# Rows of the dense part transposed by TensorE instead of VectorE, and the first block's rows kept on chip

## The chip, the core and the metric

The kernel runs on one core of one Trainium2 chip, as one launch. The metric is the device time of that launch in microseconds (us), as the median of several runs. A core has five engines that run side by side and wait for one another through semaphores: TensorE (PE in the profile; its weight loads are listed apart as PEld), VectorE (DVE), ScalarE (ACT), GpSimd (POOL) and SyncE (SP), which here only issues DMAs. PE writes to PSUM, which has eight banks of 128 x 512 floats. SBUF holds the tiles, and HBM holds the inputs, the output and the scratch tensors.

## What is computed

Two layers with the same weights, one after the other. Each is attention with 32 heads of 20 columns, then an MLP with squared ReLU. Both have a layer norm in front and a residual add behind. x is 2048 x 640 in float32, the MLP's inner width is 1536.

```python
x = x + A(layernorm(x), wqkv, wo)          # attention, 32 heads, output projection wo
x = x + B(layernorm(x), w1, b1, w2, b2)    # relu(x @ w1 + b1)**2 @ w2 + b2
x = x + A(layernorm(x), wqkv, wo)
x = x + B(layernorm(x), w1, b1, w2, b2)
```

## The kernel before

Products that need precision are made from three matmuls: each operand is split into a high part, rounded to the type that PE reads, and a low part that holds the rest. High times high, high times low and low times high are summed in PSUM. So most operands are tiles of shape [128, 2, 512]: plane 0 high, plane 1 low. `split_to` (L265) makes the two planes from a source, the high one by a cast on ACT (L267), the low one by a subtraction on DVE (L268). `THREE` (L307) names the three pairs, `chain` (L317) issues one sum of such matmuls on PE (L320).

The rows are handled in four blocks of 512 (`NQB`), each block as four tiles of 128 rows. A layer (`layer`, L1117) has these stages.

1. `qkv` (L702) and `attention` (L886): projections, scores, softmax and weighted values. Attention's own rows are normalised and transposed by `front` (L393): one PE transpose for each 128 x 128 square (L408), four of them into one PSUM bank, then a split out of PSUM. The dense part below does it in another way.
2. Output projection, `add_heads` (L1029), once for each block. For each of the four row tiles and each half of the 640 columns there is one chain of 15 matmuls into a bank, then DVE adds the bank to the residual row tile (L1044). When both halves are done, the row tile is stored to the scratch tensor `x_mid` (an issue on SP). The residual rows of the next block are loaded one block ahead (L1034).
3. MLP, `mlp` (L1069), once for each block, in two halves (`fh`) of six inner tiles. In each half: six chains of 15 matmuls from the transposed rows xnT and `w_1`; for each a ReLU on ACT (L1084), a square on DVE (L1085) and a split into h; then eight chains of 18 matmuls from h and `w_2`, each added on DVE to a row tile of the residual (L1104). That residual is loaded again from `x_mid` during the first half, and GpSimd adds `b2` to it (L1091).

Between stages 2 and 3 the rows of `x_mid` must be normalised and transposed, since the first matmuls of the MLP need them with the 640 columns on the partitions. `turned_rows` (L1048) is a generator that does this in 13 steps: load four row tiles from `x_mid`; statistics of each (`stats`, L250: L255 and L256 on DVE, L258 and L259 on GpSimd); then for each tile the normalisation (L263) and the transposition by `turned` (L284), in two steps. `turned` has 16 DVE instructions for each row tile, each of which turns five 32 x 32 squares (L292), into an SBUF tile y. `parts` (L299) splits y into xnT: for each of the five column groups a cast on ACT (L304) and a subtraction, on GpSimd or DVE in turn (L305).

The order on each engine is the order in which the program issues. `side` (L1128) takes the next step of a list and issues it; it is called after every chain of `add_heads` (8 times for a block), after every inner tile and after every chain of the second product in `mlp` (28 times for a block). So a list of steps, with `None` for an empty place, sets which work stands between which chains. Before the change, block 0's 13 steps stand in the third and fourth block of `add_heads`, and split as they go. For the other blocks the steps stand in the first half of the MLP block before, and their splits all at one place in its second half, behind the first chain of the second product (L1109).

All loads go through SP's one queue, in order (the `dma` helper, L76). The weights `w_1` (15 tiles) come in fours after each block of the projection, and its last three with `w_2` (16 tiles, L1148) after the last block; in the queue the loads of the MLP's rows stand behind them. SBUF tiles come from two rings: `arena` with 42 slots (weights, xnT, h) and `xp` with 11 row tiles (`NX`, L36), which holds x, y and r. A tile is reused when its last reader is done. PSUM banks are taken in turn (`ps_all`, L110).

Of the kernel before, what the change touches and what calls it, by code (L numbers as in the profile page):

```python
# [8 lines left out]
F32 = mybir.dt.float32  # L9
# [7 lines left out]
P = 128  # L17
# [5 lines left out]
KD = D // P  # L23
NF = F // P
QB = 512
NQB = S // QB
# [13 lines left out]
def tile_layers(  # L40
# [11 lines left out]
    nc = tc.nc  # L52
# [10 lines left out]
    def name(p):  # L63
        n_alloc[0] += 1
        return f"{p}{n_alloc[0]}"

    def slot(shape, dtype, label):
        return arena.tile(shape, dtype, tag="slot", name=name(label))

    def dma(eng, dst, src):  # L70

        if dst.dtype == F32R:
            dst = dst.bitcast(F32)
        if src.dtype == F32R:
            src = src.bitcast(F32)
        eng.dma_start(dst, src)  # L76

    def xtile(label):
        return xpool.tile([P, D], F32, tag="x", name=name(label))
# [30 lines left out]
    ps_all = Ring(0, 1, 2, 3, 4, 5, 6, 7)  # L110

    ident = cpool.tile([P, P], F32, name="ident")
# [149 lines left out]
    def normalise(eng, x, mv):  # L262
        eng.tensor_scalar(x, x, mv[:, 0:1], mv[:, 1:2], op0=ALU.subtract, op1=ALU.mult)  # L263

    def split_to(dst_hi, dst_lo, src):  # L265

        nc.scalar.copy(dst_hi, src)  # L267
        nc.vector.tensor_sub(dst_lo, src, dst_hi.bitcast(F32))  # L268
# [11 lines left out]

    def pool_lo(dst, a, b):
        nc.gpsimd.tensor_sub(dst, a, b)  # L282

    def turned(x):  # L284


        y = xtile("y")
        view = y.rearrange("p (k t) -> p k t", k=KD)
        src = x.rearrange("p (k c i) -> p c k i", k=KD, i=32)
        for a in range(4):  # L290
            for c in range(4):
                nc.vector.transpose(  # L292
                    view[32 * c : 32 * c + 32, :, 32 * a : 32 * a + 32],
                    src[32 * a : 32 * a + 32, c],
                )
            if a % 2:
                yield y

    def parts(res, i, y):  # L299

        for k, t in enumerate(res):
            cols = slice(i * P, (i + 1) * P)
            hi, lo, src = t[:, 0, cols], t[:, 1, cols], y[:, k * P : (k + 1) * P]
            nc.scalar.copy(hi, src)  # L304
            (nc.vector if k % 2 else nc.gpsimd).tensor_sub(lo, src, hi.bitcast(F32))  # L305

    THREE = ((0, 0), (0, 1), (1, 0))  # L307

    def row_tile(src, r):
        t = xtile("x")  # L310
        dma(nc.sync, t, src[r * P : (r + 1) * P, :])
        return t
# [4 lines left out]
    def chain(dst, pairs):  # L317
        last = len(pairs) - 1
        for n, (a, b) in enumerate(pairs):
            nc.tensor.matmul(dst, a, b, start=(n == 0), stop=(n == last))  # L320
# [108 lines left out]
    k_t, q_t, v_t, mx_t, kept = {}, {}, {}, {}, {}  # L429
# [596 lines left out]
        dma(q, ot.rearrange("p l t -> p (l t)"), d_o[k * P : (k + 1) * P, qb])  # L1026
        ready.setdefault(qb, {})[k] = ot

    def add_heads(qb, x_src, x_mid, xs, side):  # L1029

        ot = ready.pop(qb)
        for i in range(4):
            if qb + 1 < NQB:
                xs.append(row_tile(x_src, qb * 4 + 4 + i))  # L1034
            x = xs.pop(0)
            for hf in range(2):
                dst = ps_all("po")
                chain(dst[:, :HALF], [
                    (ot[k][:, hx, i * P : (i + 1) * P], w_o.piece(k * 4 + hw * 2 + hf))
                    for k in range(KD)  # L1040
                    for hx, hw in THREE
                ])
                c = slice(hf * HALF, (hf + 1) * HALF)
                nc.vector.tensor_add(x[:, c], dst[:, :HALF], x[:, c])  # L1044
                side()
            dma(nc.sync, x_mid[(qb * 4 + i) * P : (qb * 4 + i + 1) * P, :], x)

    def turned_rows(qb, x_src, give):  # L1048

        xs = [row_tile(x_src, qb * 4 + i) for i in range(4)]  # L1050
        yield
        mvs = []
        for x in xs:
            mvs.append(stats(x))
            yield
        for i, mv in enumerate(mvs):
            normalise(nc.vector, xs[i], mv)
            steps = turned(xs[i])
            next(steps)
            yield  # L1060
            y = next(steps)
            xs[i] = None
            give(i, y)
            yield

    def new_rows():
        return [slot([P, 2, QB], F32R, "xnT") for _ in range(KD)]

    def mlp(qb, xnt, x_mid, x_dst, side, nxt):  # L1069

        xs, res = [], None
        for fh in range(2):
            hs = []
            for f in range(fh * 6, fh * 6 + 6):
                dst = ps_all("pu")
                chain(dst, [
                    (w_1.piece(f * 10 + hw * KD + k), xnt[k][:, hx, :])
                    for k in range(KD)
                    for hw, hx in THREE
                ])  # L1080
                if qb == NQB - 1:
                    w_1.past(f * 10 + 9)
                r = xtile("r")[:, :QB]
                nc.scalar.activation(r, dst, AF.Relu, bias=b1_t[:, f : f + 1])  # L1084
                nc.vector.tensor_mul(r, r, r)  # L1085
                h = slot([P, 2, QB], F32R, "h")
                split_to(h[:, 0, :], h[:, 1, :], r)
                hs.append(h)
                if fh == 0 and f in (1, 2, 3, 4):
                    x = row_tile(x_mid, qb * 4 + f - 1)  # L1090
                    nc.gpsimd.tensor_add(x, x, b2_t)  # L1091
                    xs.append(x)
                side()
            for hf in range(2):
                c = slice(hf * HALF, (hf + 1) * HALF)
                for i in range(4):
                    dst = ps_all("y")
                    chain(dst[:, :HALF], [
                        (hs[f % 6][:, hx, i * P : (i + 1) * P], w_2.piece(at_2(f, hw, hf)))
                        for f in range(fh * 6, fh * 6 + 6)  # L1100
                        for hx, hw in THREE
                    ])
                    x = xs[i]
                    nc.vector.tensor_add(x[:, c], dst[:, :HALF], x[:, c])  # L1104
                    if fh == 1 and hf == 1:
                        r0 = (qb * 4 + i) * P
                        dma(nc.sync, x_dst[r0 : r0 + P, :], x)
                    side()
                    if (fh, hf, i) == (1, 0, 0) and nxt:  # L1109
                        res = new_rows()  # L1110
                        for j in range(4):
                            parts(res, j, nxt.pop(j))
            if fh == 0 and qb == NQB - 1:
                w_2.past(at_2(5, 1, 1))
        return res

    def layer(first, x_a, x_m, x_e, front_0, ahead):  # L1117
        qkv(first, x_a, front_0)
        xs = []
        attention(first, x_a, xs)  # L1120
        steps = []
        for i in sorted(split):
            steps += [split.pop(i), None]
        steps += [lambda: heads(nc.scalar, NQB - 1, KD - 1)]
        for k in range(KD - 1):
            heads(nc.sync, NQB - 1, k)

        def side():  # L1128
            if steps:
                (steps.pop(0) or (lambda: None))()  # L1130

        def all_steps():
            while steps:
                side()

        for qb in range(NQB):
            if qb + 2 == NQB:
                xnt = []
                norm = turned_rows(0, x_m, lambda i, y: parts(xnt, i, y))
                steps.append(lambda: xnt.extend(new_rows()))  # L1140
                steps.extend([lambda: next(norm, None)] * 13)
            add_heads(qb, x_a, x_m, xs, side)
            for s in range(qb * 4, min(qb * 4 + 4, w_1.n)):
                w_1.load(s)
            if qb + 1 == NQB:
                all_steps()
        w_o.drop()
        for s in range(w_2.n):  # L1148
            w_2.load(s)
        for qb in range(NQB):  # L1150
            rows = {}
            if qb + 1 < NQB:
                norm = turned_rows(qb + 1, x_m, rows.__setitem__)
                step = lambda norm=norm: next(norm, None)
                steps.extend([step] * 5 + [None] + [step] * 8)
            elif ahead:
                some = lambda: [next(ahead, None) for _ in range(3)]
                steps.extend([None] * 14 + [some] * 14)
            xnt = mlp(qb, xnt, x_m, x_e, side, rows if qb + 1 < NQB else None)
            if qb + 1 < NQB:  # L1160
                all_steps()
        steps.clear()
        w_1.drop()
        w_2.drop()
# [69 lines left out]
```

## Time and profile before

| | |
|---|---|
| runs | 3811.12, 3810.0 and 3806.8 us; median 3810.0 |
| profiled execution | span 3807.2 us from its first to its last instruction; the views give no other time of it |
| mean granted clock of PE | 0.985 of full speed |
| busy, share of the span | PE 97%, its weight load 55%, DVE 78%, ACT 67%, POOL 23% |
| output projection | 71.5 us in each layer |
| from the end of the projection to the end of the last layer's MLP | 387.6 us (3419.6 to 3807.2) |

The span is that of one execution, taken by the hardware profiler; it can lie beside the median of the timed runs by what one run differs from another. PE is busy for 97% of it. Nearly all of that belongs to attention, which the change doesn't touch; what matters here is what PE waits for in the short dense stages. The rows of a timeline give start and length in us, engine, line, operation, the tiles written and read, a count and, in brackets, the idle time before the instruction with what ended it. A line of the code can be that of a helper: L320 is every chain, L267 and L268 every split. Matmuls overlap, so the length of a group divided by its count is the cost of one, and the duration of a single one isn't.

### The profile page before, as it was taken

The page shows a single profiled execution, that of the slowest core. Times are in us where ns is not written, and L with a number is a line of the kernel's source. Part 1 is how long each engine was busy: PE and PEld are TensorE (multiplying, and loading weights), DVE is VectorE, ACT ScalarE, POOL GpSimd, SP SyncE. Part 2 cuts the span into 40 slices and gives each one's busy share as a digit, 9 for nine tenths or more (in the row PEclk, how much of TensorE's full clock was granted, in tenths as well). Part 3 has the DMA queues.
Part 4 walks back from the last instruction along what each step waited for, and adds up shares of the span by engine and source line. Part 5 has one row for each costly group of instructions (what it writes and reads, how often), then busy time and mean ns, then how long its engine had stood idle before and what let it go on. Part 6 is the DMA issues. An engine that isn't in the chain of part 4 may idle for free.

```text
span 3807.2 us, 64689 instructions
## 1 busy us (share of the span) xinstructions
PE 3687.9 (97%) x23412; PEld 2109.6 (55%) x23412; DVE 2974.8 (78%) x5332; ACT 2563.4 (67%) x5007; POOL 877.9 (23%) x1017
## 2 busy tenths in 40 slices
PE   7999999999999999699999999999999999997999
PEld 5677443443344338588876763434433443376888
DVE  7788999999999973666467889999999999646663
ACT  2455999999999992122214459999999999921221
POOL 6530334321221211111254201122121222111210
PEclk9999999999999999799999999999999999998999
DMA  7564454422211136311255533222222111463111
GB/s 223 187 207 144 141 156 141 140 74 79 59 47 44 43 120 237 138 42 42 90 174 181 177 126 82 74 75 59 67 77 62 43 46 42 121 236 134 42 42 42
DMA packets 257687, 404.92 MB, mean 106 GB/s; under 512 B 67708, under 2 KB 114556, under 8 KB 257368
## 3 DMA queue, kind: packets, MB, share of 16 engines
q1 hardware_dynamic: 256824, 399.08, 33.4%
q8 instruction: 185, 3.03, 0.3%
q10 hardware_dynamic: 544, 1.71, 0.1%
q14 instruction: 134, 1.10, 0.1%
HBM read 263.84 MB, written 136.81 MB: 105 GB/s over the span
## 4 chain that ended last, share of the span: by engine, by line
PE 89%; DVE 6%; DMA 2%; ACT 1%; POOL 1%; issue 1%; SPq 0%; ACTq 0%; DVEq 0%; POOLq 0%
PE banks L595 27%; PE banks L583 19%; PE banks L320 16%; PE banks L486 15%; PE banks L331 7%; PE banks L378 4%; DVE h L268 1%; DVE y L292 1%; DVE bst L255 1%; DMA x<-d_x 1%; DMA w<-d_w 1%; DVE mx L507 1%; DVE r L1085 1%; ACT h L267 1%; DVE x L263 0%
## 5 line engine op out<-in xcount | busy, mean ns | idle before, releaser
L590 ACT ACTIVATE e<-banks 128x512 f32<-128x512 f32 x4096 | 2114.5, 604 | 61.2 <-PE banks L583 3.7
L498 DVE TENSOR_REDUCE mx<-banks 128x1 f32<-128x512 f32 x2940 | 1845.7, 683 | 187.1 <-PE banks L486 116.2
L486 PE MATMUL banks<-k,q 60*128 60x512 f32 x3744 | 1154.8, 436 | 7.8 <-DMA q<-d_qk 5.3
L583 PE MATMUL banks<-q,k 62*128 62x512 f32 x4096 | 1151.8, 435 | 2.1 <-DVE mx L507 1.7
L595 PE MATMUL banks<-e,vg 128*32 128x512 f32 x8192 | 1092.2, 605 | 0.0
L583 PEld LDWEIGHTS banks<-q,k 62*128 62x128 f32 x4096 | 600.8, 185 | 699.2 <-ACT e L590 664.9
L486 PEld LDWEIGHTS banks<-k,q 60*128 60x128 f32 x3744 | 537.3, 185 | 333.6 <-DVE mx L498 206.0
L320 PE MATMUL banks<-w,h 128*128 128x320 f32 x2304 | 368.8, 320 | 48.1 <-ACT h L267 37.2
L320 PEld LDWEIGHTS banks<-w,h 128*128 128x128 f32 x2304 | 353.0, 195 | 63.0 <-ACT h L267 43.4
L320 PE MATMUL banks<-xnT,w 128*128 128x512 f32 x1440 | 334.3, 393 | 28.8 <-ACT xnT L304 28.8
L595 PEld LDWEIGHTS banks<-e,vg 128*32 128x32 f32 x8192 | 161.5, 108 | 357.9 <-issue 330.6
L518 ACT ACTIVATE rl<-banks 128x512 f32<-128x512 f32 x352 | 191.3, 596 | 246.7 <-PE banks L486 246.6
L331 PE MATMUL banks<-xnT,wqk 128*128 128x512 f32 x1200 | 322.0, 412 | 1.7 <-POOL wqk L282 1.7
L320 PEld LDWEIGHTS banks<-xnT,w 128*128 128x128 f32 x1440 | 272.1, 190 | 85.9 <-ACT xnT L304 29.3
L1084 ACT ACTIVATE r<-banks,b_t 128x512 f32<-128x512 f32 x96 | 65.9, 687 | 372.3 <-PE banks L320 245.9
L528 DVE CUSTOM_DVE_ANT_0 rl<-banks,rl 128x512 f32<-128x512 f32 x352 | 229.1, 688 | 110.8 <-PE banks L486 101.0
L507 DVE TENSOR_REDUCE mx<-banks 128x2 f32<-128x1024 f32 x226 | 271.7, 1220 | 20.0 <-PE banks L486 19.4
L331 PEld LDWEIGHTS banks<-xnT,wqk 128*128 128x128 f32 x1200 | 219.3, 192 | 86.6 <-issue 43.5
L639 POOL TENSOR_TENSOR few<-few,minus_t 128x16 f32<-128x16 f32 x62 | 179.8, 2900 | 249.8 <-DMA few<-d_s 246.1
L650 POOL TENSOR_TENSOR o<-o 128x512 f32<-128x512 f32 x62 | 79.6, 1283 | 608.7 <-DMA o<-d_r 333.6
L279 POOL CAST mr<-nt 128x32 fp32r<-128x32 f32 x64 | 13.4, 210 | 855.1 <-DVE nt L554 821.5
L267 ACT CAST h<-r 128x512 fp32r<-128x512 f32 x96 | 59.6, 620 | 186.0 <-DVE r L1085 185.3
(75 smaller groups left out, 2203.5 us busy)
## 6 DMA issues: line engine op xcount, KB each, us to landing
q<-d_qk SPq DMA_DIRECT2D x744, 80.0 KB
d_qk<-ev SPq DMA_DIRECT2D x80, 512.0 KB
k<-d_qk SPq DMA_DIRECT2D x468, 80.0 KB
x<-d_x SPq DMA_DIRECT2D x96, 320.0 KB
d_o<-ot SPq DMA_DIRECT2D x248, 80.0 KB
ot<-d_o SPq DMA_DIRECT2D x38, 512.0 KB
d_v<-v SPq DMA_DIRECT2D x32, 512.0 KB
vg<-d_v SPq DMA_DIRECT2D x32, 512.0 KB
```

What stands on the lines that cost most here:

```text
L320: nc.tensor.matmul(dst, a, b, start=(n == 0), stop=(n == last))
L331: nc.tensor.matmul(dst, w_qk.piece(pos * 10 + hw * KD + k), xt_[tb][k][:, hx, :], start=(n == 0), stop=(n == 3 * KD - 1),)
L378: nc.tensor.matmul(dst[:, :HALF], xt_[tb][k][:, hx, i * P : (i + 1) * P], w_v.piece(k * 4 + hw * 2 + hf), start=(j == 0), stop=(j == 3 * K ...
L486: nc.tensor.matmul(dst, q_t[t][b : b + 60, p, sub * P : (sub + 1) * P], k_t[t // NQB, c][b : b + 60, p, :], start=True, stop=True,)
L498: nc.vector.tensor_reduce(maxima(t)[:, 2 * p + par, sub, c : c + 1], dst, axis=AX.X, op=ALU.max)
L507: nc.vector.tensor_reduce(maxima(t)[:, 2 * p : 2 * p + 2, sub, c], dst, axis=AX.X, op=ALU.max)
L518: nc.scalar.activation(res[par], dst[:, par, :], AF.Relu)
L528: nc.vector.tensor_tensor_reduce(out=r[par], in0=dst[:, par, :], in1=r[par], scale=1.0, scalar=LEAST, op0=ALU.add, op1=ALU.max, accum_out= ...
L583: nc.tensor.matmul(dst, k_t[t // NQB, kt // 4][b : b + 62, p, (kt % 4) * P : (kt % 4 + 1) * P], q_t[t][b : b + 62, p, :], start=True, stop ...
L590: nc.scalar.activation(es[p][:, par, :], dst, AF.Exp, scale=SCALE)
L595: nc.tensor.matmul(acc[32 * h : 32 * h + 32, :], v_t[t // NQB, kt // 8][:, kt % 8, 32 * h : 32 * h + 32], es[p][:, par, :], start=(kt == 0 ...
L639: nc.gpsimd.tensor_tensor(few, few, minus_t, op=ALU.pow)
```

## The change

`turned` and `parts` go. `turned_rows` becomes a generator of 14 steps: take the rows, four statistics, four normalisations, and five steps that each transpose one column group of all four row tiles on PE, by four transposes into one bank, and split the bank into xnT with `split_to`. It is the way of `front`.

For block 0 nothing is loaded: `add_heads` keeps the four row tiles of the first block after it has stored them (`kept`), and the steps normalise these in place. They stand beside the second block of the projection (rows, four statistics, three normalisations) and the third (the last normalisation, two empty places, five transposing steps). For the other blocks the rows are loaded from `x_mid` as before, in the first steps of the MLP block ahead; the statistics keep their places, the normalisations follow, then there are twelve empty places, and the transposing steps stand behind chains 2 to 6 of the second product in the second half. `mlp` no longer returns the new rows.

```diff
-    def turned(x):
...
-    def parts(res, i, y):
...
-    def add_heads(qb, x_src, x_mid, xs, side):
+    def add_heads(qb, x_src, x_mid, xs, side, kept):
...
             dma(nc.sync, x_mid[(qb * 4 + i) * P : (qb * 4 + i + 1) * P, :], x)
+            if qb == 0:
+                kept.append(x)
...
+    def turned_rows(xs, get):
+
+        if callable(xs):
+            xs = xs()
         yield
         mvs = []
         for x in xs:
             mvs.append(stats(x))
             yield
...
+        for x, mv in zip(xs, mvs):
+            normalise(nc.vector, x, mv)
             yield
...
+        res = get()
+        for k in range(KD):
+            dst = ps_all("xt")
+            for i in range(4):
+                nc.tensor.transpose(
+                    dst[:, i * P : (i + 1) * P], xs[i][:, k * P : (k + 1) * P], ident
+                )
+            split_to(res[k][:, 0, :], res[k][:, 1, :], dst)
+            if k == KD - 1:
+                xs.clear()
             yield
...
-                    if (fh, hf, i) == (1, 0, 0) and nxt:
-                        res = new_rows()
-                        for j in range(4):
-                            parts(res, j, nxt.pop(j))
...
+        xnt, rows = [], []
         for qb in range(NQB):
             if qb + 2 == NQB:
-                xnt = []
-                norm = turned_rows(0, x_m, lambda i, y: parts(xnt, i, y))
-                steps.append(lambda: xnt.extend(new_rows()))
-                steps.extend([lambda: next(norm, None)] * 13)
-            add_heads(qb, x_a, x_m, xs, side)
+                xnt.extend(new_rows())
+            add_heads(qb, x_a, x_m, xs, side, rows)
+            if qb == 0:
+                norm = turned_rows(rows, lambda: xnt)
+                steps.extend([lambda: next(norm, None)] * 9 + [None] * 2)
+                steps.extend([lambda: next(norm, None)] * 5)
...
+                some_rows = lambda qb=qb: [row_tile(x_m, qb * 4 + 4 + i) for i in range(4)]
+                norm = turned_rows(some_rows, get)
                 step = lambda norm=norm: next(norm, None)
-                steps.extend([step] * 5 + [None] + [step] * 8)
+                steps.extend([step] * 9 + [None] * 12 + [step] * 5)
...
-            xnt = mlp(qb, xnt, x_m, x_e, side, rows if qb + 1 < NQB else None)
+            mlp(qb, xnt, x_m, x_e, side)
+            xnt = new
```

More of the change, by code (lines that the diff above doesn't have):

```diff
@@ L282, in pool_lo @@
         nc.gpsimd.tensor_sub(dst, a, b)
-    def turned(x):
[L287 to L297, printed above, removed]
-    def parts(res, i, y):
[L301 to L305, printed above, removed]
     THREE = ((0, 0), (0, 1), (1, 0))
@@ L1046, in add_heads @@
             dma(nc.sync, x_mid[(qb * 4 + i) * P : (qb * 4 + i + 1) * P, :], x)
-    def turned_rows(qb, x_src, give):
-        xs = [row_tile(x_src, qb * 4 + i) for i in range(4)]
+            if qb == 0:
[3 more added lines that the diff above has]
+            xs = xs()
         yield
@@ L1055, in turned_rows @@
             yield
[L1056 to L1059, printed above, removed]
+        for x, mv in zip(xs, mvs):
+            normalise(nc.vector, x, mv)
             yield
-            y = next(steps)
-            xs[i] = None
-            give(i, y)
+        res = get()
[8 more added lines that the diff above has]
+                xs.clear()
             yield
@@ L1067, in new_rows, with mlp @@
         return [slot([P, 2, QB], F32R, "xnT") for _ in range(KD)]
-    def mlp(qb, xnt, x_mid, x_dst, side, nxt):
-        xs, res = [], None
+    def mlp(qb, xnt, x_mid, x_dst, side):
+        xs = []
         for fh in range(2):
@@ L1108, in mlp @@
                     side()
-                    if (fh, hf, i) == (1, 0, 0) and nxt:
-                        res = new_rows()
-                        for j in range(4):
-                            parts(res, j, nxt.pop(j))
             if fh == 0 and qb == NQB - 1:
                 w_2.past(at_2(5, 1, 1))
-        return res
     def layer(first, x_a, x_m, x_e, front_0, ahead):
@@ L1150, in layer, with get @@
         for qb in range(NQB):
-            rows = {}
+            new = []
             if qb + 1 < NQB:
-                norm = turned_rows(qb + 1, x_m, rows.__setitem__)
+                def get(new=new):
+                    new.extend(new_rows())
+                    return new
+                some_rows = lambda qb=qb: [row_tile(x_m, qb * 4 + 4 + i) for i in range(4)]
+                norm = turned_rows(some_rows, get)
                 step = lambda norm=norm: next(norm, None)
-                steps.extend([step] * 5 + [None] + [step] * 8)
+                steps.extend([step] * 9 + [None] * 12 + [step] * 5)
             elif ahead:
```

## The prediction

> **What bounds the kernel now.** I read first where TensorE (PE) isn't busy in the two dense parts. This is the table of busy time by stretch, cut at the output projection, the change to the MLP and the rest of each layer; the columns are length, then busy time of PE, its weight load, DVE, ACT and POOL, the granted clock, the DMA share and GB/s.
>
> ```profile
> 1452.49:1524.02 71.53, 71.53 (x485) 70.79 (x482) 36.00 (x83) 2.82 (x11) 5.79 (x14) 1.00 0.68 241
> 1524.02:1584.92 60.90, 28.08 (x107) 21.52 (x106) 31.06 (x66) 9.73 (x22) 13.31 (x18) 0.71 0.55 215
> 1584.92:1895.15 310.23, 301.30 (x1643) 271.84 (x1644) 193.57 (x412) 66.83 (x147) 50.62 (x72) 0.98 0.13 44
> ...
> 3348.11:3419.64 71.53, 71.53 (x485) 70.78 (x482) 37.08 (x86) 2.82 (x11) 5.79 (x14) 1.00 0.71 257
> 3419.64:3478.26 58.62, 28.02 (x105) 21.47 (x106) 29.98 (x63) 9.73 (x22) 13.32 (x18) 0.74 0.57 223
> ```
>
> The projection keeps PE full (71.53 of 71.53). Then comes a hole: 60.90 - 28.08 = 32.8 us of idle PE in the first layer, 58.62 - 28.02 = 30.6 us in the second. After it PE is nearly full again. So time can be had only in the hole, and PE work added elsewhere in a dense part is paid in full. The timeline of PE shows what the first hole waits for (start, length, and in brackets the idle time before it and its releaser):
>
> ```profile
> 1455.26 68.76 PE L320 MATMUL banks<-wo,ot 128*128 128x320 f32 x465
> 1538.99 22.76 PE L320 MATMUL banks<-xnT,w 128*128 128x512 f32 x90 [14.97 <-ACT xnT L304]
> 1561.60 1.04 PE L320 MATMUL banks<-w,h 128*128 128x320 f32 x6
> 1571.34 1.36 PE L320 MATMUL banks<-w,h 128*128 128x320 f32 x3 [8.71 <-ACT h L267]
> ...
> 1584.92 15.29 PE L320 MATMUL banks<-w,h 128*128 128x320 f32 x83 [1.61 <-ACT h L267]
> ```
>
> There are two waits, one behind the other. The first, 14.97 us, is for the transposed rows xnT. The second runs from 1562.6 to 1584.92 and is for h. The timelines of DVE and of the SP queue (which issues the DMAs in order) say why:
>
> ```profile
> 1535.82 2.79 DVE L292 STREAM_TRANSPOSE y<-x 32x160 f32<-32x160 f32 x8
> 1539.17 0.91 DVE L305 TENSOR_TENSOR xnT<-y,xnT 128x128 fp32r<-128x128 f32 x2 [0.56 <-ACT xnT L304]
> 1540.01 0.88 DVE L1044 TENSOR_TENSOR x<-banks,x 128x320 f32<-128x320 f32 x2
> ...
> 1568.95 0.89 DVE L255 BATCH_NORM_STATS2 bst<-x 128x6 f32<-128x320 f32 x2 [17.96 <-DMA x<-d_x]
> ```
>
> ```profile
> 1518.71 22.52 SPq L76 DMA_DIRECT2D d_x<-x  x4
> 1541.32 16.76 SPq L76 DMA_DIRECT2D w<-d_w  x19
> 1558.92 9.56 SPq L76 DMA_DIRECT2D x<-d_x  x8
> ```
>
> DVE is late with its transposes, so the last residual add of the projection (L1044) ends at 1540.89, although PE was through at 1455.26 + 68.76 = 1524.02. SP holds the store of that row until then. Behind it stand 19 weight loads and behind those the rows of the next block, whose statistics (L255) DVE waits for until 1568.95; the squares and splits that make h queue behind that wait. **The second wait thus hangs on the same late add as the first**, through the DMA queue. The second layer has the same chain (PE, DVE, SP, PE):
>
> ```profile
> 3350.88 68.76 PE L320 MATMUL banks<-wo,ot 128*128 128x320 f32 x465
> ```
>
> ```profile
> 3434.49 0.88 DVE L1044 TENSOR_TENSOR x<-banks,x 128x320 f32<-128x320 f32 x2
> ...
> 3462.28 0.89 DVE L255 BATCH_NORM_STATS2 bst<-x 128x6 f32<-128x320 f32 x2 [16.85 <-DMA x<-d_x]
> ```
>
> ```profile
> 3435.81 16.37 SPq L76 DMA_DIRECT2D w<-d_w  x19
> ```
>
> ```profile
> 3478.26 20.98 PE L320 MATMUL banks<-w,h 128*128 128x320 f32 x129 [1.61 <-ACT h L267]
> ```
>
> **The change, part by part.** First the price of a transpose on PE. The kernel has them already, where attention's rows are transposed (L408); from the chain of waits, then from the list of that line's instructions (min/median/max in ns):
>
> ```profile
> 1891.03 0.87 PE banks L408 x8
> ...
> 1909.56 1.31 PE banks L408 x12
> ...
> 1946.87 0.44 PE banks L408 x4
> ```
>
> ```profile
> L408 PE MATMUL banks<-ident,x x160: 270/273/477, 12.3 to 1948.4; 128*128 128x128 f32 x160
> ```
>
> Eight take 0.87 us, twelve 1.31, four 0.44: 0.109 us each, with matmuls on either side. One block of rows has 5 x 4 = 20, so 2.18 us of PE, eight blocks 17.4 us. A single instruction lasts 273 ns, but they overlap; I take the spacing and keep 0.27 for a rival.
>
> The Trainium skill (TensorE: Matmul & The Clock Gate, Part 4: PE-mode transpose) speaks against the change: it gives a transpose about 275 ns within a kernel. The trace agrees with that as a duration (273 ns) and not as a cost per transpose (0.109 us); by the page's figure the sum would be the first rival's below.
>
> *Projection.* The first block's rows stay on chip, so their statistics need no load; statistics and normalisation fall beside the second block, 20 transposes into the third. DVE loses 64 block transposes (86.0 us in the four blocks of a layer by the grouped rows, 256 x 336 ns) and keeps up with PE as it did before them:
>
> ```profile
> L292 DVE STREAM_TRANSPOSE y<-x 32x160 f32<-32x160 f32 x256 | 86.0, 336 | 4.1
> ```
>
> ```profile
> 1495.46 0.49 DVE L1044 TENSOR_TENSOR x<-banks,x 128x320 f32<-128x320 f32 x1 [1.71 <-PE banks L320]
> ```
>
> Then PE ends at 1524.02 + 2.18 = 1526.20, and the last add 0.49 later, at 1526.7 instead of 1540.89: **14.2 us earlier**. In the second layer 3419.64 + 2.18 + 0.49 = 3422.3 instead of 3435.37: **13.1 us earlier**. The 19 weight loads and the row loads shift by as much, since nothing else held SP at that point. So the statistics start at 1554.8 and 3449.2 and PE resumes 14.2 and 13.1 us earlier, at 1570.7 and 3465.2. PE's first wait goes, and **the second grows**: the first half of the MLP now starts at 1526.2, takes 20.59 us as in the warm block below, and h is then late until the rows have landed. Of the 63.4 us of idle PE some 36 stay; the loads are the next late thing, at the rate of this row (last column, GB/s), so they can't close up:
>
> ```profile
> 1545.00:1560.00 15.00, 15.00 (x67) 12.39 (x66) 2.77 (x4) 3.13 (x5) 0.00 (x0) 1.00 1.02 410
> ```
>
> *MLP.* In blocks 0, 1 and 2 of each layer 20 transposes stand among the second half's chains, where PE is the bound:
>
> ```profile
> 1606.79 20.59 PE L320 MATMUL banks<-xnT,w 128*128 128x512 f32 x90
> 1627.22 2.93 PE L320 MATMUL banks<-w,h 128*128 128x320 f32 x17
> 1630.33 18.89 PE L320 MATMUL banks<-w,h 128*128 128x320 f32 x127 [0.17 <-DVE h L268]
> ```
>
> That is 6 x 2.18 = **13.1 us added**. What goes there (DVE's transposes, 20 ACT casts and 20 subtractions per block) I cost at nothing: PE didn't wait for it, only 0.17 us here. What comes is five ACT casts and five DVE subtractions per block:
>
> ```profile
> L267 ACT CAST xnT<-banks x20: 580/587/607, 15.0 to 1914.0; 128x512 fp32r<-128x512 f32 x20
> L268 DVE TENSOR_TENSOR xnT<-banks,xnT x20: 676/690/692, 15.7 to 1914.6; 128x512 fp32r<-128x512 f32 x20
> ```
>
> The last pair, with an add before it, is done 0.49 + 0.59 + 0.69 = 1.8 us after the transposes; two chains of 18 (18 x 18.89 / 127 = 2.68 us each) hide it. Without that cover each of the six blocks would lose the 1.8 us, 10.6 in all.
>
> *New waits.* PE's transposes wait for DVE's normalisation, and every matmul queues behind them. In the projection the last normalisation is three chains ahead (6.6 us), in the MLP over twelve: no wait. DVE's normalisation in place waits for the row's store, and the adds queue behind it; and four row loads leave SP's queue:
>
> ```profile
> 1471.78 0.32 SPq L76 DMA_DIRECT2D d_x<-x  x1
> ...
> 1492.17 2.11 SPq L76 DMA_DIRECT2D x<-d_x  x4
> ```
>
> The first block's last store leaves at 1471.78; the first normalisation stands behind the sixth chain of the second block, some six times 2.2 us later: no wait. The loads' 2.11 us fell where SP waits for adds anyway: nothing. The statistics in the first half of blocks 1 and 2 stay where they are, and so do their stalls:
>
> ```profile
> 1672.44 0.42 PE L320 MATMUL banks<-w,h 128*128 128x320 f32 x1 [0.75 <-DVE h L268]
> 1674.68 0.56 PE L320 MATMUL banks<-w,h 128*128 128x320 f32 x2 [1.83 <-ACT h L267]
> ```
>
> **Sum:** -14.2 - 13.1 + 13.1 = -14.2 us. The profiled execution's span is 3807.2 us:
>
> ```profile
> span 3807.2 us, 64689 instructions
> ```
>
> The median of the runs, 3810.0, stands 2.8 us above that span, within what the runs differ by (3806.8 to 3811.12). The change gives 3793.0 of span, **3796 us** at the median. Bounds: if half of the stalls of about 2.6 us in four MLP blocks go with DVE's load, 5 us less; if each of the 40 groups of transposes adds a hand-over stall of 0.17 us, 7 us more: 3791 to 3803.
>
> **The rivals.**
>
> *Transposes don't overlap.* At 0.27 us each they cost 160 x 0.27 = 43.2 us against 14.2 + 13.1 + 2 x 2.18 = 31.7 us won without them: 11.5 us slower, **3822**. For it: the 273 ns, and only four stand together. Against it: four in 0.44. It decides from 31.7 / 160 = 0.198 us on. Chance 0.06.
>
> *The wait moves to the weight loads (slower).* The ring for rows has 11 tiles; the kept rows hold four, four more are loaded ahead, one is in work. Should a row load on SP have to wait for a freed tile, everything behind it on SP is held, the weights too. If they start no sooner than now, PE resumes at 1584.92 and 3478.26 as before and only the 13.1 us in the MLP are left: **3823**. For it: SP is in order, and its loads stand behind its stores. Against it: two tiles are spare, and a freed one's store is three rows old. It decides where SP is held over 7 us a layer past the last add. Chance 0.08.
>
> *Both waits go.* Were the rows there when the first half ends, all 63.4 us of idle would go, less 17.4 for the transposes: 46 us, **3764**. Against it: 19 loads of about half a megabyte stand ahead of the rows, at 410 GB/s. Chance 0.03.
>
> *Half is given back* through small stalls at the transposes: about **3803**. Chance 0.07.
>
> **How the numbers follow.** The forecast has 0.76. A measurement of this kernel tells about 0.2% (7.6 us) from no change. Faster: the forecast nearly whole, the third rival, a little of the last, 0.80. Same: most of the last, 0.07. Slower: the first two, 0.13. The range, 3787 to 3807, takes the forecast's bounds, a measurement's scatter of some 4 us and the last rival.
>
> **What would show it.** PE's wait for xnT behind the projection is gone in both layers; the last L1044 ends within a microsecond of PE's last matmul there; the 19 weight loads leave SP about 14 and 13 us earlier relative to the projection's start; DVE's wait for x<-d_x is over 18 us; and blocks 0 to 2 of the MLP last about 2.2 us longer. It is wrong if the weight loads don't move, if a group of four transposes takes over 0.8 us, or if PE waits for DVE at a transpose.

## The result, and the profile after the change

The changed kernel takes **3799.8 us** against 3808.7 before (medians of 11 runs each). The ratio is 0.9975, with a 95% interval from 0.9966 to 0.9984: 9.5 us faster, between 6.1 and 13.0. Forecast were 14.2 us; the direction and the two terms of the sum hold, and the size is a third smaller. The profiled execution has a span of 3799.7 us.

The changed kernel's busy time by stretch, cut as in the prediction (projection; hole; rest of the layer's dense part, in the first layer up to the same chains; then the second layer's first two):

```profile
1451.35:1524.89 73.54, 73.54 (x505) 73.03 (x503) 29.91 (x56) 3.55 (x6) 2.97 (x8) 1.00 0.65 228
1524.89:1569.98 45.09, 25.90 (x107) 20.04 (x105) 16.43 (x25) 7.54 (x12) 10.55 (x12) 0.80 0.71 275
1569.98:1889.79 319.81, 310.64 (x1703) 280.99 (x1704) 130.83 (x211) 64.50 (x102) 32.69 (x36) 0.96 0.12 42
...
3343.39:3416.93 73.54, 73.54 (x505) 73.03 (x503) 29.91 (x56) 3.55 (x6) 2.97 (x8) 1.00 0.64 226
3416.93:3461.05 44.12, 25.91 (x108) 20.05 (x106) 16.36 (x25) 7.54 (x12) 10.55 (x12) 0.79 0.72 281
```

The projection is 2.0 us longer (73.54 against 71.53), the holes are 15.8 and 14.5 us shorter, and the rest of the first layer's dense part is 9.6 us longer (319.81 against 310.23). PE, then DVE, then SP in the first hole:

```profile
1524.89 20.59 PE L297 MATMUL banks<-xnT,w 128*128 128x512 f32 x90
1545.32 1.04 PE L297 MATMUL banks<-w,h 128*128 128x320 f32 x6
1556.29 1.36 PE L297 MATMUL banks<-w,h 128*128 128x320 f32 x3 [9.93 <-ACT h L267]
...
1569.98 21.81 PE L297 MATMUL banks<-w,h 128*128 128x320 f32 x129 [1.61 <-ACT h L267]
```

```profile
1525.09 0.49 DVE L1021 TENSOR_TENSOR x<-banks,x 128x320 f32<-128x320 f32 x1 [1.71 <-PE banks L297]
...
1553.89 0.89 DVE L255 BATCH_NORM_STATS2 bst<-x 128x6 f32<-128x320 f32 x2 [19.18 <-DMA x<-d_x]
```

```profile
1512.41 13.52 SPq L76 DMA_DIRECT2D d_x<-x  x4
1526.03 17.76 SPq L76 DMA_DIRECT2D w<-d_w  x19
1544.58 8.84 SPq L76 DMA_DIRECT2D x<-d_x  x8
```

The wait for xnT is gone: the MLP starts where the projection ends. The last add (L1021 now) follows PE at once. The 19 weight loads leave SP 74.7 us after the projection's start instead of 88.8, 14.1 us sooner. And DVE's wait for the rows of block 1 has grown from 17.96 to 19.18 us, with PE idle for 19.2 us behind it. All four were forecast. The second layer does the same: its weight loads leave SP 74.7 us after the projection's start instead of 87.7, and DVE's wait has grown from 16.85 to 18.27 us. The transposes in the MLP's second halves stand between chains without a wait:

```profile
1615.16 3.05 PE L297 MATMUL banks<-w,h 128*128 128x320 f32 x19 [0.17 <-DVE h L268]
1618.05 0.60 PE L1043 MATMUL banks<-ident,x 128*128 128x128 f32 x4
1618.41 2.89 PE L297 MATMUL banks<-w,h 128*128 128x320 f32 x18
```

To see which stretch lost the missing microseconds I cut PE's timeline of every kernel at the same four places. A row gives one profiled execution, in us; "to the second half" runs from the projection's start to the start of block 0's second half, both layers added; "first halves" is the mean length of the second product in the first halves of blocks 1 and 2 (four), "second halves" that in blocks 0 to 2 (six); "dense" runs from the projection's start to block 3's second half, both layers.

| kernel | to the second half | first halves | second halves | dense | median of the runs |
|---|---|---|---|---|---|
| before | 305.3 | 26.35 | 21.84 | 830.3 | 3808.7 |
| before, again | 306.5 | 26.44 | 21.84 | 831.9 | 3812.5 (one) |
| changed | 279.5 | 27.34 | 24.01 | 821.7 | 3799.8 |
| changed, again | 278.9 | 26.97 | 24.01 | 819.5 | 3801.5 (one) |
| changed, third | 279.2 | 26.44 | 24.01 | 817.8 | 3798.2 (one) |
| projection part alone | 280.4 | 26.50 | 21.83 | 806.0 | 3783.0 |
| MLP part alone | 307.9 | 26.02 | 24.00 | 844.7 | 3827.7 |
| changed, late statistics | 231.6 | 21.84 | 24.01 | 751.7 | 3729.3 |
| changed, without b2 | 268.7 | 21.91 | 24.01 | 789.0 | 3767.7 (one) |
| changed, rows ahead of w_2 | 231.6 | 27.47 | 24.00 | 774.3 | 3753.8 |
| late, MLP rows on VectorE | 231.8 | 21.83 | 27.53 | 773.0 | 3753.0 |
| before, late statistics | 260.3 | 21.84 | 33.22 | 835.7 | 3814.2 |
| late, VectorE's pieces spread | 231.8 | 21.83 | 21.89 | 739.1 | **3716.2** |

By the means of the first five rows the change takes 26.7 us off the first stretch (forecast 27.3), adds 2.17 us to each of six second halves (forecast 2.18), and the four first halves are 0.5 us longer each (not forecast). Dense: 11.5 us shorter.

### The profile page after: what moved, and what is told of

Its sections match the earlier page's. It is cut to its first block, busy times and chain, and to the rows that moved or that the text cites. A ratio compares the mean times of both kernels' runs of the same rounds, so it can differ in the third digit from the quotient of the medians.

```text
span 3799.7 us, 64213 instructions
## 1 busy us (share of the span) xinstructions
PE 3705.0 (98%) x23572; PEld 2130.6 (56%) x23572; DVE 2807.6 (74%) x4796; ACT 2556.0 (67%) x4887; POOL 831.0 (22%) x921
## 4 chain that ended last, share of the span: by engine, by line
PE 91%; DVE 4%; DMA 2%; ACT 1%; POOL 1%; issue 0%; SPq 0%; ACTq 0%; POOLq 0%; DVEq 0%
PE banks L572 27%; PE banks L560 20%; PE banks L297 18%; PE banks L463 15%; PE banks L308 6%; PE banks L355 4%; DVE h L268 1%; DVE mx L484 1%; DVE bst L255 1%; DMA w<-d_w 1%; DVE r L1070 1%; ACT h L267 1%; PE banks L385 0%; PE banks L1043 0%; DMA x<-d_x 0%
## 5 line engine op out<-in xcount | busy, mean ns | idle before, releaser
L297 PE MATMUL banks<-w,h 128*128 128x320 f32 x2304 | 380.0, 323 | 51.6 <-ACT h L267 40.1
L484 DVE TENSOR_REDUCE mx<-banks 128x2 f32<-128x1024 f32 x226 | 271.7, 1220 | 20.0 <-PE banks L463 19.2
L1089 DVE TENSOR_TENSOR x<-banks,x 128x320 f32<-128x320 f32 x128 | 62.8, 491 | 216.5 <-PE banks L297 216.5
```

The lines of the kernel that those rows point to most:

```text
L484: nc.vector.tensor_reduce(maxima(t)[:, 2 * p : 2 * p + 2, sub, c], dst, axis=AX.X, op=ALU.max)
```

## The experiments

**1. The two kernels once more, for the scatter** (no edit; twice the changed kernel, once the kernel before).

> A second profiled execution of the changed kernel. Theory 1 (about 5 us of the expected 14 are lost in the MLP, in every execution: the transposes cost 2.18 us a block as forecast, but the wait for h in the first halves of blocks 1 and 2 is longer, because GpSimd's addition of b2 meets one more of VectorE's subtractions, and PE's clock then comes back later): from the first to the last product of the first half in blocks 1 and 2 again 27.2 to 27.6 us, and four subtractions of about 2.07 us instead of three. Rival (scatter: the clock's windows fell badly in one execution): at least two of the four such stretches at 26.0 to 26.5 us, as in the kernel before. Time 3796 to 3803.

> A second profiled execution of the kernel before. Theory 1: the same four stretches again at about 26.0 to 27.1 us with waits for h of 0.75 to 1.5 us ahead of the 1.83. Rival (scatter): some of them at 27.3 or more. Both: the hole behind the projection 60.9 and 58.6 us long within half a microsecond. Time 3806 to 3812.

> A third profiled execution of the changed kernel, for the clock. Theory 1 as amended by the first runs (a wait for h of about 3 us drops PE's clock to half for one or for two of its steps of 3.4 us, and only the two-step cases cost the 0.8 us that the changed kernel lost per block): each of the four first halves is either near 26.4 us with one step of half clock or near 27.4 with two. Systematic: again three or four of four with two steps. Scatter: two or fewer.

The four stretches are, in the changed kernel, 27.34, 27.54, 27.15, 27.34; again 27.41, 26.70, 26.17, 27.58; third 27.26, 27.41, 26.42, 24.67. In the kernel before they are 26.19, 27.08, 26.13, 26.00 and 26.90, 26.20, 26.71, 25.94. So theory 1 fell in its strict form: it isn't so in every execution. Its cause, one more slowed subtraction, shows in eight of the twelve stretches after the change and in two of the eight before (a fourth subtraction over 1 us), but PE's idle time there is nearly the same by the means, 3.03 us against 2.98. What splits the values is the clock. These are the windows around the first such wait, before the change and after it (PE's clock is the column after the five engines):

```profile
1669.48:1675.41 5.93, 3.19 (x19) 2.43 (x17) 4.47 (x7) 1.83 (x3) 3.35 (x5) 1.00 0.00 0
1675.41:1678.80 3.39, 3.39 (x16) 3.39 (x17) 2.77 (x8) 0.00 (x0) 0.00 (x0) 0.64 0.02 5
1678.80:1682.29 3.49, 3.49 (x22) 3.49 (x22) 3.04 (x9) 0.00 (x0) 0.00 (x0) 0.86 0.00 0
```

```profile
1656.50:1662.26 5.76, 2.63 (x17) 2.13 (x15) 4.36 (x8) 1.82 (x3) 3.66 (x5) 0.88 0.00 0
1662.26:1665.14 2.88, 2.88 (x10) 2.65 (x11) 2.20 (x4) 0.00 (x0) 0.00 (x0) 0.50 0.00 0
1665.14:1668.56 3.42, 3.42 (x17) 3.42 (x16) 0.35 (x1) 0.00 (x0) 0.00 (x0) 0.62 0.00 0
1668.56:1671.97 3.41, 3.41 (x26) 3.41 (x25) 1.68 (x4) 0.00 (x0) 0.00 (x0) 1.00 0.00 0
```

Both waits last some 3 us. Before the change the clock is at half for one step of 3.4 us behind the wait, after it for two (10 and 17 matmuls in windows of 2.9 and 3.4 us, where the full pace is 26 in 3.4). Over all profiles of the two kernels, all eight waits before have one step; of the twelve after, eight have two steps, three have one and one has none. One step costs about 1.6 us beyond the idle time, two about 2.45 (the stretch less 21.84 us and less PE's idle time). The third execution has two of four, which was laid down as scatter; the means differ by 0.5 us. Whether the changed kernel's waits fall worse on the clock's steps as a rule, or fell so in these executions, stays open: of the versions below, the projection part alone has one step at each of its four waits, the MLP part alone has one at three and none at the fourth, and the kernel with the rows ahead of w_2 has two at each of four.

Two expectations for the kernel before were missed by a little: it took 3812.5 us where 3812 was the most, and its second hole is 59.45 us long where 58.6 within half a microsecond was expected. So executions of one kernel differ by some 0.9 us in that hole.

**2. Each half of the change alone.** Block 0 by the new way and the other blocks by the old one, and the reverse:

```diff
# projection part alone, from the kernel before
+            if qb == 0:
+                kept.append(x)
...
-                norm = turned_rows(0, x_m, lambda i, y: parts(xnt, i, y))
+                norm_0 = turned_on_pe(first_four, lambda: xnt)
# MLP part alone, from the changed kernel
-                norm = turned_rows(rows, lambda: xnt)
+                norm_0 = turned_on_dve(0, x_m, lambda i, y: parts(xnt, i, y))
```

> The change in the projection alone: the first block's rows are kept and transposed by PE, the other blocks' rows go by VectorE as before. Theory 1 (and the prediction's first term): the hole shortens by 13.8 and 12.5 us and the MLP stays as before: 26 us faster than before, about 3782. Scatter as the cause of the shortfall: the same 3782, so this run tests the size of the term alone. Rival (VectorE's relief in the MLP is part of the gain): clearly less than 20 us faster.

> The change in the MLP alone: block 0 by VectorE as before, the other blocks by PE. Prediction's second term alone: 13.1 us slower than before, 3822. Theory 1: 13.1 us and about 4 more in blocks 1 and 2, 3826. Rival (VectorE's relief in the MLP is worth something): under 10 us slower.

The projection part alone is 24.7 us faster in the medians (ratio 0.9938, from 0.9921 to 0.9954), its dense part 25.1 us shorter. The first term is confirmed alone, and the version beats the changed kernel. The MLP part alone is 19.9 us slower (ratio 1.0056, from 1.0041 to 1.0071). In its profile the dense part is 13.6 us longer, all of it in the six second halves and the hole; the first halves, at 26.02, lose nothing, which speaks once more against theory 1. The prediction's second term, 13.1 us, is thus confirmed in the profile, and the median is 6.8 us beyond it. That execution took 3823.9 us and two others 3831 and 3834; what those two lost is in no trace.

**3. What the waits that are left hang on.** The first halves' waits stand behind statistics that DVE does between the subtractions for h; beside them GpSimd adds b2. First the statistics of the next block's rows, and the normalisations, are moved behind the first half's second product:

```diff
-                steps.extend([step] * 9 + [None] * 12 + [step] * 5)
+                steps.extend([step] + [None] * 5 + [step] * 8 + [None] * 7 + [step] * 5)
```

> The changed kernel with the statistics of the next block's rows moved out of the MLP's first inner tiles: they and the normalisations stand behind the eight chains of the first half's second product, the transposes stay. Theory 2 (what is left of the hole, 19.2 and 18.2 us of idle PE, is VectorE waiting in order for the rows of block 1 with the work on h behind it, and the waits of some 3 us in blocks 1 and 2 are the statistics ahead of h; the half clock follows from the waits): all first halves take about 21.9 us, no wait for h over 0.3 us, no half clock inside the MLP: 37 us of idle, some 4 us of half clock behind it and 4 x 5.4 us in blocks 1 and 2 go, about 3737. Rival (the weights themselves are late, so PE waits for w_2 behind the projection): the hole shrinks by less than 10 us a layer, 3770 or more.

It took 3729.3 us, 2.03% less than before (0.9797, from 0.9781 to 0.9814), and 8 us less than I expected. Block 0's first half now runs without a gap, though its rows stand where they stood in the queue:

```profile
1527.14 20.59 PE L297 MATMUL banks<-xnT,w 128*128 128x512 f32 x90
1547.57 2.94 PE L297 MATMUL banks<-w,h 128*128 128x320 f32 x17
1550.68 18.89 PE L297 MATMUL banks<-w,h 128*128 128x320 f32 x127 [0.17 <-DVE h L268]
1569.41 20.59 PE L297 MATMUL banks<-xnT,w 128*128 128x512 f32 x90
```

So the 37 us of idle PE were not the weights' doing: w_2 was there. They were the statistics' place in DVE's order, where DVE waited for rows that nobody needed yet. Most of the 8 us beyond my number lie here too: the stretch up to block 0's second half is 47.6 us shorter in the table, both layers added, where I had counted 41 for it, with 2 us of half clock a layer. Then GpSimd's addition is taken out of the changed kernel, with the statistics left in place; its output lacks b2:

```diff
-                    nc.gpsimd.tensor_add(x, x, b2_t)
```

> The changed kernel without GpSimd's addition of b2, so the output lacks b2 (that part is left out). Theory 2a (the subtractions of 2.07 us are slowed by GpSimd's addition beside them): all 48 subtractions for h in a layer take about 0.69 us, the waits for h in blocks 1 and 2 fall under 0.3 us, the half clock there goes, and behind the rows' landing PE resumes some 5 us sooner: 5 x 2 + 5.4 x 4 = 30 us faster, about 3770. Rival (the statistics alone make the wait): less than 10 us faster, waits of 2 us or more remain.

3767.7 us in its one run, near the 3770 of theory 2a. Three of the four first halves of blocks 1 and 2 took 21.84 us and one 22.11. None of its 96 subtractions for h takes over 0.70 us; in the changed kernel 23 take over 1. DVE in block 1 of the changed kernel (square, subtraction, statistics), then in block 1 without the addition:

```profile
1647.87 0.64 DVE L1070 TENSOR_TENSOR r<-r 128x512 f32<-128x512 f32 x1
1649.19 2.07 DVE L268 TENSOR_TENSOR h<-r,h 128x512 fp32r<-128x512 f32 x1 [0.69 <-ACT h L267]
1651.18 0.87 DVE L255 BATCH_NORM_STATS2 bst<-x 128x6 f32<-128x320 f32 x2
```

```profile
1641.51 0.69 DVE L1070 TENSOR_TENSOR r<-r 128x512 f32<-128x512 f32 x1 [0.29 <-ACT r L1069]
1642.89 0.69 DVE L268 TENSOR_TENSOR h<-r,h 128x512 fp32r<-128x512 f32 x1 [0.69 <-ACT h L267]
1643.50 0.88 DVE L255 BATCH_NORM_STATS2 bst<-x 128x6 f32<-128x320 f32 x2
```

An inner tile costs PE 3.4 us. On DVE it is square, ACT's cast and subtraction, 0.69 each, then 1.1 of statistics: 3.2. The subtraction beside GpSimd's add takes 2.07 instead of 0.69, and the sum is some 4.5. Either alone fits, both together don't: moving the statistics or dropping the addition each empties the wait.

**4. The rows' place in the queue.** Block 1's rows are loaded ahead of w_2, and the statistics stay:

```diff
+        first_rows = [row_tile(x_m, 4 + i) for i in range(4)]
         for s in range(w_2.n):
             w_2.load(s)
...
```

> The changed kernel with block 1's four row loads issued ahead of the sixteen w_2 loads instead of behind them; the statistics stay where they are. Theory 2: the rows are there about 20 us sooner, VectorE doesn't wait, PE's idle time behind the first half falls from 19 us to 3 or less in each layer: about 33 us faster, 3767; blocks 1 and 2 keep their 27 us. Rival (w_2 or the residual rows are what PE really waits for): under 10 us faster, with the wait now named for a weight load or for the residual rows.

3753.8 us (0.9858, from 0.9843 to 0.9873), 46 us below the changed kernel where I expected 33; blocks 1 and 2 keep their 27 us. The SP queue, and PE:

```profile
1529.14 1.39 SPq L76 DMA_DIRECT2D w<-d_w  x3
1530.58 2.03 SPq L76 DMA_DIRECT2D x<-d_x  x4
1532.66 17.50 SPq L76 DMA_DIRECT2D w<-d_w  x16
```

```profile
1528.01 20.59 PE L297 MATMUL banks<-xnT,w 128*128 128x512 f32 x90
1548.43 2.94 PE L297 MATMUL banks<-w,h 128*128 128x320 f32 x17
1551.54 18.90 PE L297 MATMUL banks<-w,h 128*128 128x320 f32 x127 [0.17 <-DVE h L268]
```

Block 0's first product of the second kind falls from 46.3 us to 21.85: 19 us of idle, and 5 more of half clock behind it, which I had left out there.

**5. Where VectorE's transposes would fit.** With late statistics nothing waits for DVE, and PE's 2.16 us a block are paid in full. So the MLP's rows went back to DVE, in pieces of four block transposes; block 1's rows and block 0's residual rows are loaded ahead of w_2:

```diff
# from the projection part alone
...
-                steps.extend([step] * 5 + [None] + [step] * 8)
+                two = lambda norm=norm: [next(norm, None) for _ in range(2)]
+                steps.extend([step] + [None] * 5 + [step] * 4 + [two] * 4 + [step] * 8)
...
```

> The projection part of the change, with the MLP's rows turned by VectorE again, in pieces of four block transposes spread over the free places; statistics late as in the run with late statistics, and block 1's rows and block 0's residual rows loaded ahead of the sixteen w_2 loads. Theory (in the MLP TensorE is the bound and VectorE isn't, so the 2.16 us a block of PE transposes are a loss there once nothing waits for VectorE): 13 us faster than with late statistics, 3716, second halves back at 21.84 us. Rival (VectorE is then full: about 3.4 us of its work for each 3.43 us of PE in the second half's first tiles): new waits for h, 3729 or slower, with the half clock back.

The rival held: 3753.0 us (0.9854, from 0.9837 to 0.987), second halves at 27.53. DVE between two inner tiles, and PE's wait at the end:

```profile
1579.09 1.38 DVE L292 STREAM_TRANSPOSE y<-x 32x160 f32<-32x160 f32 x4
1580.51 0.69 DVE L1107 TENSOR_TENSOR r<-r 128x512 f32<-128x512 f32 x1
1581.88 0.69 DVE L268 TENSOR_TENSOR h<-r,h 128x512 fp32r<-128x512 f32 x1 [0.69 <-ACT h L267]
1582.61 1.38 DVE L292 STREAM_TRANSPOSE y<-x 32x160 f32<-32x160 f32 x4
```

```profile
1596.50 21.80 PE L319 MATMUL banks<-w,h 128*128 128x320 f32 x129 [2.90 <-ACT h L267]
```

From piece to piece it takes 3.52 us, and PE needs 3.4 a tile: DVE never catches up on what it brought along. A coarser form of the same mistake is the kernel before with late statistics and its turning steps simply behind them:

```diff
-                steps.extend([step] * 5 + [None] + [step] * 8)
+                steps.extend([step] + [None] * 5 + [step] * 12)
```

> The kernel before with nothing changed but the place of the statistics: behind the first half's second product, and the turning steps one after the other from there. Theory 2 (the statistics' place and not the transposes makes the wait for h): the hole keeps PE's first wait of 15 and 14 us for the transposed rows and loses the second, blocks 1 and 2 lose their waits: 35 us of idle, 4 of half clock and 4 x 4.5 us go, 3752, if the turning steps that now reach into the second half's first tiles cost nothing there. Rival (they do): some 10 us more, with waits for h in the second halves.

3814.2 us (1.0013, from 1.0004 to 1.0022), far from both numbers. The first halves come out at 21.84 us and the hole keeps its first wait, 15 and 14 us, as forecast; the second halves of blocks 0, 1 and 2 take 36.8, 31.0 and 31.8 us instead of 21.84, 34 us a layer. The waits had only moved:

```profile
1611.12 1.36 PE L320 MATMUL banks<-w,h 128*128 128x320 f32 x3 [4.30 <-ACT h L267]
1616.04 1.36 PE L320 MATMUL banks<-w,h 128*128 128x320 f32 x3 [3.56 <-ACT h L267]
1618.02 22.04 PE L320 MATMUL banks<-w,h 128*128 128x320 f32 x129 [0.62 <-ACT h L267]
```

Last, three of DVE's small pieces are taken from the second half's first tiles and put behind its chains (the split of the last row tile moves behind them):

```diff
# from the kernel with the pieces at every tile
...
-                steps.extend([step] + [None] * 5 + [step] * 4 + [two] * 4 + [step] * 8)
+                steps.extend([step] + [None] * 5 + [step] * 4 + [two] * 4 + [None, step] * 3 + [step] * 5)
```

> The run before last (projection by PE, MLP rows by VectorE, late statistics, early row loads) with three of VectorE's pieces taken from the second half's first tiles and put behind its chains; the split of the last row tile follows them. Theory (there the pieces only fell in the wrong place: 0.69 + 0.69 + 0.69 + 1.4 us for each tile is just over PE's 3.43; with a piece at every other tile VectorE catches up): second halves at 21.9 us, no half clock in the MLP, 3716, so PE's 2.16 us a block are a loss once the pieces are placed well. Rival (VectorE has no room for 21.5 us of transposes a block wherever they stand): second halves over 24 us, 3729 or slower, so PE's transposes are the cheaper ones.

**3716.2 us**, 2.46% below the kernel before (0.9754, from 0.9738 to 0.9771), and below every other. Against the changed kernel with late statistics (3729.3) that is 13 us, and the profiles show where: the six second halves take 21.89 us instead of 24.01. The order of the loads differs too, but the stretch that it bears on is the same in both, 231.8 and 231.6 us. One step of half clock is left in the MLP, in the first layer's block 3, where none was expected. The second half of block 0 has no wait but the usual 0.17:

```profile
1590.65 2.94 PE L319 MATMUL banks<-w,h 128*128 128x320 f32 x17
1593.75 18.89 PE L319 MATMUL banks<-w,h 128*128 128x320 f32 x127 [0.17 <-DVE h L268]
1612.48 20.59 PE L319 MATMUL banks<-xnT,w 128*128 128x512 f32 x90
```

## Why the prediction was right, and where its sum was off

- **The hole follows the late add.** Right. The projection's last add comes with PE's end, the weight loads move up by 14.1 us in the first layer, and the two layers gain 13.9 and 12.8 us up to block 0's second half by the means (14.2 and 13.1 forecast). The projection part alone shows this term by itself.
- **PE's transposes at 0.109 us.** Right: 2.17 us a block, 13.0 in all, where 13.1 were forecast. The rival of transposes that don't overlap is refuted: a group of four lasts 0.60 us by its ends, but the next chain starts 0.36 us after it.
- **"The statistics in the first half of blocks 1 and 2 stay where they are, and so do their stalls."** This is the term of the sum that was mis-sized: it stood at nothing, and these first halves took 0.5 us more each by the means, 2.1 us in all. The waits themselves stayed at some 3 us; what grew is the time lost behind them at half clock, from 1.6 to 2.05 us by the means. I had read a stall as its idle time alone; the half clock behind it costs more than half as much again, and not the same each time. That the change brings this about, and not the executions that were profiled, isn't shown.
- **The sum.** -26.7 + 13.0 + 2.1 = -11.6 us in the traces (from the table's dense column -11.5) against -14.2 forecast, and 9.5 by the ratio of the runs, whose interval ends at 13.0, short of the forecast. The spans of the same five profiles differ by 10.4 us. The 2 us between trace and ratio lie within what executions differ by; they are assigned to no stage.
- **DVE's work in the MLP "at nothing".** Right as placed, and shown by the MLP part alone, where taking it away wins nothing. But it is so only because other waits covered DVE's. Once those are gone, its place decides: 3716 us with the pieces spread, 3753 with the pieces at every tile.
- **The rivals.** The weight loads did move, so that rival fell too. "Half is given back" comes near in its time (3803), but not in its cause: the second halves grew by 2.17 us where the transposes alone were to cost 2.18, so there are no stalls at the transposes. "Both waits go" wasn't what the change does, but it can be had: 3764 was its price, and issuing the row loads ahead of w_2 gives 3753.8. I had held the 19 loads ahead of the rows for given; they are an order that a few lines change.

## What to carry to other kernels

When an engine is late, follow its last output through the DMA queue too: here one late add held back weights, and behind them rows, statistics and a second wait. A gain read off one wait comes back in part as the next wait on the same chain, so ask what that one really needs; statistics for the next block needed no place ahead of this block's h. And count a stall of TensorE with the half clock behind it, not as its idle time alone.

## What the runs showed of the hardware

- *The clock.* Where PE's granted clock drops in the dense parts of these profiles, it goes to half for one to eight whole steps of 3.41 us (3.41 to 27.31 us), behind waits of 3 us as well as behind long ones; in the changed kernel with late statistics it doesn't drop between the projection and block 3's second half. Each wait of 3 us is one of 0.7 to 1.5 us and one of 1.83, a matmul apart. In the changed kernel three such waits of nearly the same size were followed by different numbers of steps: 0.97 and 1.83 us by two, 0.95, 1.83 and 0.17 by one, and 0.76, 1.83 and 0.17 by none. The Trainium skill (TensorE: Matmul & The Clock Gate, Part 1: The HAM clock gate) says that the clock is set by a free-running window of 3413 ns with half speed as the idle state; the traces agree with both. That a wait's price depends on where it falls in the window would explain the three cases, and is not shown.
- *Transposes.* The Trainium skill (TensorE: Matmul & The Clock Gate, Part 4: PE-mode transpose) says that full clock doesn't engage for transposes. With four at a time between chains of 18 matmuls the clock stayed at 1.00 here (1612.05 to 1636.07 us in the changed kernel), and a group added 0.36 us.
- *VectorE beside GpSimd.* A subtraction of two SBUF tiles took 0.69 us alone and 2.07 beside GpSimd's addition of 1.56 us. The Trainium skill (SBUF — State Buffer, SBUF: two separate sides) calls the port that the two share an exclusive lock, and the waiting engine fully blocked; the 1.38 us more agree with a wait for most of the addition.
